# Loading the first sixteen token rows of the input in transfers of 64 partitions instead of 32, with the first four rows asked for in two parts

## The chip, the core and the metric

The kernel runs on one core of a Trainium2 chip. A core has TensorE (PE, matrix products into PSUM), VectorE (DVE), ScalarE (ACT), GpSimd (POOL) and SyncE (SP, which here does nothing but issue transfers). Each engine runs its own instructions strictly in the order in which they stand, and waits on semaphores for the others. Transfers between HBM and SBUF run on 16 DMA engines that SP's and POOL's transfers share. The metric is the device time of one execution in microseconds (us).

## What is computed

The reference is a block of two parts over 2048 tokens of 448 channels, in float32: an S4D state space layer (a long convolution whose kernel K is built from complex exponentials) and an MLP that mixes tokens, each behind an adaptive layer norm:

```python
x = A_u                                            # (1, 2048, 448)
mod = (_silu(c) @ w_mod).reshape(1, 6, 1, -1)      # sa, ca, ga, sb, cb, gb
h = _layernorm(x) * (1 + ca) + sa
# S4D: dt = exp(log_dt), A = -exp(log_A_real) + 1j*A_imag, C = (C_real + 1j*C_imag)*dt
#      K = 2 * real(sum_n C * exp(A * dt * pos)); y = causal convolution of h with K, + h*D_skip
x = x + ga * S4D(h)
h = _layernorm(x) * (1 + cb) + sb
x = x + gb * (W2 gelu(W1 h^T + b1) + b2)^T
```

## The kernel before

The work has three stages. The first, some 300 us, builds the convolution kernel for 28 groups of 16 channels (56 half groups `s`), two halves `s` per group; in windows of eight half groups, beside it, the input is normalised and taken through two stages of a Fourier transform. The second multiplies and transforms back. The third is the MLP, in which PE is busy without a gap.

The parameters of the first 128 channels go through `first_chain` (on DVE, ACT and POOL): it makes exponents and phases, splits each into a rounded float32 part and a rest (`split`: a cast and a subtraction, on POOL or DVE), and SP copies the pieces into the tiles `lex` (exponents, four tiles) and `lph` (phases, three tiles) that PE multiplies with a table `tab`. `direct(ha, lex, r, g)` (L911) is one such copy of 32 KB into rows r to r+32 of tile g. The later parameters go through DRAM: `chain(q)` stores its splits to `pars` (L404) and `load_up` (L616) and `load_lo` (L620) read them back into `lex` and `lph` by group. L620 takes two of the three parameters, so that its source has an outermost extent of two.

In window 0 PE makes the exponents of half groups 0 to 7 (`st_exponents`, L630, into PSUM `xe` and `xg`), ACT takes exp of them (L659). Then, per half group, `st_phase` (PE, L630), sines on ACT (L692 to L698), products with the magnitudes on POOL (`G`, L700 and L701) and DVE (`E`, L702 to L706), and 64 small products of `G` and `E` on PE (`st_kgen`, L727). PE's phases for half group s+2 go into the PSUM tile that DVE has finished reading for s (L706).

The input `A_u` is read once as `xt`: partition p holds 16 consecutive tokens (rows 0 to 15 of the tile), each of 448 floats. `x_load(r0, n)` (L310) brings rows r0 to r0+n: rows 0 to 3 from POOL in `first_chain`, rows 4 to 7 from SP behind the parameters, rows 8 to 11 and 12 to 15 in the half groups 1 and 2, one half of the partitions from SP and one from POOL. DVE takes mean and variance of each row (`u_stats`, L527). In window 8 PE multiplies the rows with a table (L555), DVE writes the results to one of three `yt` tiles (L558, two instructions to a tile) and SP stores each tile to `yu_d` (L560); a `yt` tile can be written again when its store has landed.

SP's queue also carries the modulation weights (`wm_load`, L337, 784 KB each). It is in the written order up to half group 8; behind that a scheduler orders SP's transfers, while the other four engines keep the order of the code throughout. At most eight of SP's transfers are under way: each takes one of eight semaphores in turn, and SP waits until the transfer eight places ahead has landed.

Of the kernel before, what the change touches and what calls it, by code (L numbers as in the profile page):

```python
# [21 lines left out]
L, D, N, F = 2048, 448, 256, 1792  # L22
# [210 lines left out]
def tile_adaln_s4d_mixer(ctx, tc, i, out):  # L233
    nc = tc.nc
    x = i["A_u"][0]
# [17 lines left out]
    with ExitStack() as es:  # L253
        V, S, G, T = nc.vector, nc.scalar, nc.gpsimd, nc.tensor
# [50 lines left out]
        xt = xp.tile([P, 16, D + 2], F32, name="xt")  # L305

        def x_load(r0, n, eng=nc.sync):
            for g in range(4):
                to = xt[32 * g : 32 * g + 32, r0 : r0 + n, 0:D]
                (nc.sync if r0 > 7 and g < 2 else eng).dma_start(to, x.rearrange("(s n h r) d -> h s n r d", s=2, h=2, r=16)[g // 2, g % 2, :, r0 : r0 + n])  # L310


        mg = cg.tile([P, 2, P], BF16, name="mg")
# [9 lines left out]
        lex = [cg.tile([P, N], F32R, name=f"lex{k}") for k in range(4)]  # L323
# [21 lines left out]
        for q in range(4):  # L345
            r = slice(32 * q, 32 * q + 1)
# [542 lines left out]
        def first_chain():  # L889
            cr, ci, a, aim = (raws[0][nm] for nm in ("A_C_real", "A_C_imag", "A_log_A_real", "A_A_imag"))  # L890
            xa, ya, s, t, u, ph, p64 = (
                qp.tile([P, N], F32, tag=nm, name=nm) for nm in ("xa", "ya", "s", "t", "u", "ph", "p64")
            )
# [3 lines left out]
            def split(eng, src):  # L897

                hl = room.pop()
                eng.tensor_copy(hl[:, 0].bitcast(F32R), src)  # L900
                eng.tensor_tensor(hl[:, 1].bitcast(F32R), src, hl[:, 0], ALU.subtract)
                return hl
# [6 lines left out]
            def direct(hl, tile, r, g):  # L909

                nc.sync.dma_start(tile[g][r : r + 32].bitcast(F32), hl[16 * g : 16 * g + 16])  # L911
# [18 lines left out]
            ha = split(G, a)  # L930
            tt(ya, ya, xa, ALU.mult)
            ts(t, s, 2.0**-40, 2.0**80, ALU.is_lt, ALU.mult)
            stt(p64, t, 1.0, s, ALU.max, ALU.mult)
            for g in range(4):
                direct(ha, lex, 0, g)
                if g < 3:
                    direct(ha, lex, 64, g)
            x_load(0, 4, G)
            S.activation(u, ya, AF.Square)
            S.activation(u, u, AF.Ln, bias=1.0)  # L940
            S.activation(p64, p64, AF.Ln)
# [12 lines left out]
            hs = split(V, s)  # L954
            for g in range(4):
                direct(hs, lex, 96, g)
                if g == 2:
                    direct(ha, lex, 64, 3)
            tt(ph, ph, w, ALU.subtract)
            hp = split(G, ph)  # L960
            direct(hp, lph, 0, 0)
# [9 lines left out]
            tt(xa, xa, u, ALU.subtract)  # L971
            hl = split(G, p64)
            direct(hl, lph, 64, 0)
            hc = split(V, xa)
            direct(hc, lph, 96, 0)
            store(ha, (0, 1), (1, 1))
# [3 lines left out]
            store(hc, (2, 0))  # L980

        first_chain()
        par_load(1, par_names[2:4])
        for g in (1, 2):
            load(g, False)
        x_load(4, 2)
        x_load(6, 2)
        wm_load(1, wm_slot(1))
        remainder()
# [254 lines left out]
        n = pieces[0]  # L1244
# [47 lines left out]
        for k in range(NP + 1):  # L1292

            n = NP + k
# [27 lines left out]
            if k in (2, 4):  # L1322
                r = k // 2 - 1
# [13 lines left out]
    with ExitStack() as es:  # L1337
        es.enter_context(tc.manual_schedule(engines={ENG.PE, ENG.Activation, ENG.DVE, ENG.Pool}))
        V, S, G = nc.vector, nc.scalar, nc.gpsimd
# [167 lines left out]
        for t in range(16):  # L1507
            ss = slice(t * P, (t + 1) * P)
            xt = ru.tile([P, D], F32, tag="x2", name="x2")
            nc.sync.dma_start(xt, x2_d[ss])  # L1510
            o = pacc.tile([P, D], F32, tag="acc", name="o")
            for kh in range(2):
                n = 32 + 2 * t + kh
# [38 lines left out]
```

## Time and profile before

| | us |
|---|---|
| median of three runs | 665.27 |
| lowest, highest | 664.42, 666.83 |
| the profiled execution, as timed | 667.08 |
| its span in the profile | 665.3 |
| what lies around the span | 1.78 |
| TensorE's granted clock, mean | 0.991 |

The profile is of one execution. The span counts from its first instruction. Rows of a timeline give start, duration, engine, line, operation, tiles and count, and in brackets the idle time of the engine ahead of it with what ended it; rows of the chain give start, duration and what the end was waiting for there. "SPq" is SP's queue of transfers: the duration is that of issuing, not of the transfer.

### The profile page before, as it was taken

Reading aid. Unit: us, or ns where it says so; the run is one execution under the profiler, and the core shown is the slowest. Engines: PE = TensorE matmul, PEld = TensorE weight load, DVE = VectorE, ACT = ScalarE, POOL = GpSimd, SP = SyncE. Lnnn points to the kernel's source line nnn. Section 1 sums busy time; section 2 is a strip of 40 time slices with the busy share of each in tenths; the row PEclk is TensorE's granted clock in tenths of the full one; section 3 lists DMA queues with packets and bytes.
Section 4 is the critical chain, followed back from the end, with each engine's and each line's share of the span. In section 5 each row is a group of like instructions: output and inputs, shape, how many; then the busy total and the mean of one; then the engine's idle time right before and its main releaser. Section 6 shows DMA issues by size and latency. Waiting matters only on the chain.

```text
span 665.3 us, 19255 instructions
## 1 busy us (share of the span) xinstructions
PE 614.8 (92%) x7686; PEld 445.0 (67%) x7686; DVE 445.5 (67%) x850; ACT 441.1 (66%) x828; POOL 269.8 (41%) x349
## 2 busy tenths in 40 slices
PE   1868999999998999989999899999999999999997
PEld 0534555445455565655655567788999999999997
DVE  8996899889895686859766678787522553333331
ACT  6978598999989999999678588886222532222220
POOL 7884679579499778787564000000000000000000
PEclk9999999999999899999999999999999999999999
DMA  6695647599684467576688999936664265555540
GB/s 160 191 220 146 220 171 243 223 219 285 199 292 152 132 140 207 162 199 202 204 275 273 253 245 248 230 112 203 179 182 142 66 192 163 165 161 163 160 119 29
DMA packets 99602, 125.16 MB, mean 188 GB/s; under 512 B 13780, under 2 KB 81144, under 8 KB 99512
## 3 DMA queue, kind: packets, MB, share of 16 engines
q1 hardware_dynamic: 98568, 121.30, 64.1%
q0 software_dynamic: 944, 2.62, 1.7%
q8 instruction: 61, 1.00, 0.7%
q14 instruction: 29, 0.24, 0.1%
HBM read 88.53 MB, written 34.87 MB: 185 GB/s over the span
## 4 chain that ended last, share of the span: by engine, by line
PE 64%; ACT 11%; DMA 8%; DVE 7%; issue 5%; POOL 4%; SPq 1%; ACTq 0%; POOLq 0%; DVEq 0%
PE o L1518 7%; PE o L1520 7%; PE o L1519 7%; PE xe L630 6%; PE acc L1355 6%; PE acc L1357 6%; PE acc L1356 6%; PE kg L727 5%; PE xg L630 4%; DMA w<-in_B_w_dram 3%; PE vv L858 3%; ACT mag L659 2%; DMA v_d<-vt 2%; PE kx L835 2%; POOL G L700 2%
## 5 line engine op out<-in xcount | busy, mean ns | idle before, releaser
L218 ACT CAST whi<-w 128x896 fp32r<-128x896 f32 x64 | 59.7, 938 | 136.2 <-PE o L1519 82.6
L227 DVE TENSOR_TENSOR wlo<-w,whi 128x896 fp32r<-128x896 f32 x64 | 68.1, 1086 | 40.8 <-ACT whi L218 40.8
L700 POOL TENSOR_TENSOR G<-mag,gs 128x512 f32<-128x512 f32 x56 | 71.9, 1283 | 37.9 <-ACT gs L696 37.9
L1355 PE MATMUL acc<-h3h,whi 128*128 128x448 f32 x224 | 83.0, 371 | 2.3 <-ACT h3h L1428 1.1
L1356 PE MATMUL acc<-h3l,whi 128*128 128x448 f32 x224 | 81.1, 362 | 0.6 <-DVE h3l L1429 0.4
L1518 PE MATMUL o<-uh,whi 128*128 128x448 f32 x224 | 81.3, 363 | 0.0
L1357 PE MATMUL acc<-h3h,wlo 128*128 128x448 f32 x224 | 81.3, 363 | 0.0
L1520 PE MATMUL o<-uh,wlo 128*128 128x448 f32 x224 | 81.2, 362 | 0.0
L1519 PE MATMUL o<-ul,whi 128*128 128x448 f32 x224 | 80.6, 360 | 0.0
L727 PEld LDWEIGHTS kg<-E,G 128*32 128x32 f32 x3584 | 54.7, 111 | 35.7 <-issue 20.6
L727 PE MATMUL kg<-E,G 128*32 128x64 f32 x3584 | 64.8, 222 | 9.0 <-issue 6.4
L701 POOL TENSOR_TENSOR G<-mag,gs 128x512 f32<-128x512 f32 x56 | 71.9, 1284 | 0.0
L630 PE MATMUL xg<-tab,lph 64*128 64x512 f32 x112 | 62.1, 555 | 6.4 <-DVE E L706 4.5
L630 PE MATMUL xe<-tab,lph 64*128 64x512 f32 x112 | 62.3, 557 | 0.6 <-ACT xg L698 0.3
L1523 DVE TENSOR_TENSOR y<-o,x 128x448 f32<-128x448 f32 x16 | 10.0, 624 | 78.9 <-PE o L1520 78.9
L680 POOL TENSOR_TENSOR m<-mag,w 128x512 f32<-128x512 f32 x53 | 55.7, 1051 | 4.2
L1355 PEld LDWEIGHTS acc<-h3h,whi 128*128 128x128 f32 x224 | 42.0, 188 | 15.1 <-ACT h L1427 2.8
L1356 PEld LDWEIGHTS acc<-h3l,whi 128*128 128x128 f32 x224 | 41.9, 187 | 4.2 <-DVE h3l L1429 0.9
L1520 PEld LDWEIGHTS o<-uh,wlo 128*128 128x128 f32 x224 | 42.1, 188 | 3.2
L1357 PEld LDWEIGHTS acc<-h3h,wlo 128*128 128x128 f32 x224 | 42.0, 188 | 3.2
L1519 PEld LDWEIGHTS o<-ul,whi 128*128 128x128 f32 x224 | 41.9, 187 | 2.9
L702 DVE TENSOR_TENSOR E<-m,xe 128x512 f32<-128x512 f32 x53 | 36.1, 682 | 11.3 <-issue 3.3
(249 smaller groups left out, 1405.6 us busy)
## 6 DMA issues: line engine op xcount, KB each, us to landing
w<-in_B_w_dram SPq DMA_DIRECT2D x64, 224.0 KB
w<-in_B_w_dram SPq DMA_DIRECT2D x32, 448.0 KB
yu_d<-yt SPq DMA_DIRECT2D x16, 448.0 KB
yi<-yu_d SPq DMA_DIRECT2D x32, 224.0 KB
us_d<-uo SPq DMA_DIRECT2D x16, 448.0 KB
u<-us_d SPq DMA_DIRECT2D x64, 112.0 KB
v_d<-vt SPq DMA_DIRECT2D x32, 224.0 KB
vt<-v_d SPq DMA_DIRECT2D x14, 448.0 KB
```

The lines of the kernel that those rows point to most:

```text
L218: self.nc.scalar.copy(hi, w)
L227: eng.tensor_tensor(lo, w, hi.bitcast(F32), ALU.subtract)
L630: T.matmul(out[k], lhs[r], rhs[r], start=start, stop=stop)
L700: G.tensor_tensor(Gt[:, 1], mg_, v32(sg), ALU.mult)
L701: G.tensor_tensor(Gt[:, 0], mg_, v32(cg_), ALU.mult)
L727: T.matmul(kg[32 * q : 32 * q + 32, m], Gt[:, c, d], E[:, c, d], start=h == 0 and c == 0 and m == 0, stop=h == 1 and c == 1, skip_group_ch ...
L1355: nc.tensor.matmul(acc[f], hi[:, fs], h3h[:, r], start=r == 0, stop=False)
L1356: nc.tensor.matmul(acc[f], hi[:, fs], h3l[:, r], start=False, stop=False)
L1357: nc.tensor.matmul(acc[f], lo[:, fs], h3h[:, r], start=False, stop=r == 15)
L1518: nc.tensor.matmul(o, hi[:, ks], uh[kh][:, k], start=kh == 0 and k == 0, stop=False)
L1519: nc.tensor.matmul(o, hi[:, ks], ul[kh][:, k], start=False, stop=False)
L1520: nc.tensor.matmul(o, lo[:, ks], uh[kh][:, k], start=False, stop=kh == 1 and k == 6)
```

## The change

`x_load` makes two transfers of 64 partitions instead of four of 32; the tokens that land in each partition are the same. Rows 0 to 3, asked for in one call before, are asked for as rows 0 and 1 at the old place and rows 2 and 3 behind `hl = split(G, p64)`, POOL's last split. The copies of the first split `ha` into `lex` tile 3 (rows 0 and 64) both go out among the copies of `hs` (row 96); one of them stood ahead of these.

```diff
         def x_load(r0, n, eng=nc.sync):
-            for g in range(4):
-                to = xt[32 * g : 32 * g + 32, r0 : r0 + n, 0:D]
-                (nc.sync if r0 > 7 and g < 2 else eng).dma_start(to, x.rearrange("(s n h r) d -> h s n r d", s=2, h=2, r=16)[g // 2, g % 2, :, r0 : r0 + n])
+            for h in range(2):
+                to = xt[64 * h : 64 * h + 64, r0 : r0 + n, 0:D]
+                (nc.sync if r0 > 7 and h == 0 else eng).dma_start(to, x.rearrange("(n h r) d -> h n r d", h=2, r=16)[h, :, r0 : r0 + n])
...
-            for g in range(4):
+            for g in range(3):
                 direct(ha, lex, 0, g)
-                if g < 3:
-                    direct(ha, lex, 64, g)
-            x_load(0, 4, G)
+                direct(ha, lex, 64, g)
+            x_load(0, 2, G)
...
             for g in range(4):
                 direct(hs, lex, 96, g)
-                if g == 2:
-                    direct(ha, lex, 64, 3)
+                if g in (1, 2):
+                    direct(ha, lex, 64 * g - 64, 3)
...
             hl = split(G, p64)
             direct(hl, lph, 64, 0)
+            x_load(2, 2, G)
```

On SP near the start, the copies into `lex` (lex_142 to lex_145 are tiles 0 to 3; the row of two for lex_144 is its copies of `ha`, the single rows of lex_142 and lex_143 are those of `hs`):

```order
 L911 DMA lex_143<-wm_79 32x1x256 x2
 L911 DMA lex_144<-wm_79 32x1x256 x2
-L911 DMA lex_145<-wm_79 32x1x256
 L911 DMA lex_142<-wm_79 32x1x256
 L911 DMA lex_143<-wm_79 32x1x256
+L911 DMA lex_145<-wm_79 32x1x256
 L911 DMA lex_144<-wm_79 32x1x256
```

The copy of `hs` into tile 0 moves up one place, that of `ha` into tile 3 goes back two.

On SP some twenty places on, the input rows 4 to 7 (2x448), the weights (wm_79) and the first halves of rows 8 to 11 and 12 to 15 (4x448), with the phases that are read back for later groups:

```order
-L310 DMA xt<-in_A_u_dram 32x2x448 x8
+L310 DMA xt<-in_A_u_dram 64x2x448 x4
 L337 DMA wm_79<-in_w_mod_dram 112x4x448
-L310 DMA xt<-in_A_u_dram 32x4x448 x2
+L310 DMA xt<-in_A_u_dram 64x4x448
 L616 DMA lph_139<-pars_57 32x256
 L620 DMA lph_139<-pars_57 64x1x256
-L310 DMA xt<-in_A_u_dram 32x4x448 x2
+L310 DMA xt<-in_A_u_dram 64x4x448
```

Twelve transfers become six; what stands between them stays.

On SP in window 8, where the scheduler orders, the stores of the second chain's splits (pars_58 from `hl`), the stores of `yt`, and loads for later:

```order
 L404 DMA pars_58<-hl 128x512 x2
+L291 DMA A_log_A_real<-in_A_log_A_real_dram 64x128 x2
+L616 DMA lex_142<-pars_58 32x256
 L560 DMA yu_d<-yt 128x896
 L404 DMA pars_58<-hl 128x512
-L560 DMA yu_d<-yt 128x896
-L616 DMA lex_142<-pars_58 32x256
+L616 DMA lex_143<-pars_58 32x256
+L560 DMA yu_d<-yt 128x896
+L620 DMA lex_142<-pars_58 64x1x256
```

Two loads from `pars_58`, which need the stores of it that stand just ahead to have landed, now stand ahead of the first and second store of `yt`; loads of raw parameters for the last chain (L291) have come forward from a place some twenty rows on.

## Prediction

> **What bounds the kernel now.** I read the page first, then the chain of waits from 0 to 80 us, then the timelines of DVE, POOL, SP and PE over the same time, and last the DMA engines by stretches. The page's busy times and its chain:
>
> ```profile
> PE 614.8 (92%) x7686; PEld 445.0 (67%) x7686; DVE 445.5 (67%) x850; ACT 441.1 (66%) x828; POOL 269.8 (41%) x349
> PE 64%; ACT 11%; DMA 8%; DVE 7%; issue 5%; POOL 4%; SPq 1%; ACTq 0%; POOLq 0%; DVEq 0%
> ```
>
> PE sets the whole, but the change lies where PE does not: its transfers are issued in the first 40 us. What it is worth is what still stands of a shift when PE, behind that stage, carries it to the end. The chain of the start:
>
> ```profile
> 12.43 0.59 SPq L911
> ...
> 13.07 1.86 DMA lex<-wm
> 14.93 0.78 PE xg L630
> ...
> 15.77 7.44 ACT mag L659 x15
> ...
> 29.83 0.66 DVE E L705
> 30.49 0.61 DVE E L706
> ...
> 44.71 4.38 issue
> ```
>
> The copy of `hs` into tile 0 is issued at 12.43 and lands at 14.93; ACT's exponentials start with it. At 29.83 the chain goes over from ACT to DVE. At 44.71 stands the largest wait of the stage: PE stops for 4.38 us in the middle of 64 equal products and no semaphore shows. DVE's rows of the same stretch, and two further on:
>
> ```profile
> 10.61 0.42 DVE L901 TENSOR_TENSOR wm<-s,wm 128x256 fp32r<-128x256 f32 x1
> ...
> 14.85 1.15 DVE L971 TENSOR_TENSOR xa<-xa,u 128x256 f32<-128x256 f32 x1
> ...
> 27.09 0.67 DVE L702 TENSOR_TENSOR E<-m,xe 128x512 f32<-128x512 f32 x1
> ...
> 33.89 0.69 DVE L702 TENSOR_TENSOR E<-m,xe 128x512 f32<-128x512 f32 x1 [0.41 <-ACT xe L695]
> ...
> 45.80 0.68 DVE L706 TENSOR_TENSOR E<-wm,xg 128x512 f32<-128x512 f32 x1
> ...
> 74.94 1.27 DVE L558 SCALAR_TENSOR_TENSOR yt<-pu,mod 128x448 f32<-128x448 f32 x2
> ...
> 108.40 1.28 DVE L558 SCALAR_TENSOR_TENSOR yt<-pu,mod 128x448 f32<-128x448 f32 x2 [0.79 <-DMA yu_d<-yt]
> ```
>
> No row between 4.24 and 33.89 has a bracket: DVE works without a gap there, so what ACT gains ahead of 29.83 reaches nobody unless DVE gets faster too.
>
> **The start.** `hs` is split at 11.03 (10.61 and 0.42), yet its copy is issued at 12.43: SP is at its older copies.
>
> ```profile
> L911 SPq DMA_DIRECT2D lex<-wm x12: 567/590/725, 7.0 to 14.4; - x12
> DMA  0003897979993989999997212227614999999992
> 20.00:25.00 5.00, 5.00 (x17) 2.72 (x17) 4.86 (x8) 4.97 (x10) 4.69 (x8) 1.00 0.91 320
> ```
>
> The first is the group of these twelve issues, median 0.59 us; one goes back behind `hs`, so its first copy leaves about 0.6 us earlier. The second is the DMA engines' busy share in 40 slices of 0 to 25 us: full up to 13.1 us, at a fifth from 13.75 to 16.9. Half of the first four input rows, 0.46 MB, moves out of the full part into the idle one, and the copy may land sooner than the 1.86 us of the chain. At 320 GB/s, the last row's rate and the best of this stage, these bytes are 1.4 us, of which I take 0.7. So ACT starts 0.6 to 2.0 us earlier; I take 1.3. The copies into tile 3 go later by one or two places, but of ACT's sixteen exponentials, 7.44 us, the last four need it, some 5 us after the first: no cost.
>
> POOL's side:
>
> ```profile
> 6.91 2.27 POOL L310 DMA_DIRECT2D xt<-in_A_u_dram  x4
> ...
> 13.42 0.78 POOL L901 TENSOR_TENSOR wm<-p,wm 128x256 fp32r<-128x256 f32 x1
> 14.17 0.42 POOL L675 TENSOR_TENSOR w<-mag 128x16 f32<-128x16 f32 x1
> 14.66 1.06 POOL L680 TENSOR_TENSOR m<-mag,w 128x512 f32<-128x512 f32 x1
> 16.92 0.24 POOL L675 TENSOR_TENSOR w<-mag 128x16 f32<-128x16 f32 x1 [1.20 <-ACT mag L659]
> ...
> 32.35 1.11 POOL L310 DMA_DIRECT2D xt<-in_A_u_dram  x2
> 72.87 0.40 POOL L398 CAST hl<-ph 128x256 fp32r<-128x256 f32 x1 [0.80 <-DMA pars<-hl]
> ```
>
> Two issues cost 1.11 (half of the first row is 1.14). At the old place they leave a hole, since the cast of `ph` waits for DVE anyway. At the new one they stand ahead of the product at 14.66, which then ends at 16.85, and the 1.20 us of idle time ahead of 16.92 hide that. Without that cover it would be 1.1 us on POOL, and DVE's first E product has its operand from here only at 27.09, so nothing would show. One DVE row profits: L971 took 1.15 beside POOL's product at 14.66 and ends with it, where the same size takes 0.42 at 10.61. With transfers issued there instead, 0.73 us of DVE's unbroken row is saved, if the product, now later, does not hold up another DVE instruction for as long. Bounds 0 and 0.73 each; I take 0.7, because the next DVE instructions are small ones. By 31 us the shift is thus -0.7, not -1.3.
>
> The Trainium skill has a rule that speaks against this edit. SBUF — State Buffer, "SBUF: two separate sides", warns that a transfer issued from GpSimd stalls while VectorE runs two-port operations, since GpSimd then can't write descriptors; its example is 620 ns that become 3100. By that rule the two issues among L971 and its neighbours could hold POOL for some 5 us more, an estimate from that page's figures, and the sum would be up to 4 us higher. No row here shows it: the 1.11 us at 32.35 lie beside DVE's E products and the 2.27 at 6.91 beside its first chain, so I give it no chance of its own.
>
> Rows 2 and 3 are asked for 7 us later. Their use is the first row below, the time of POOL's eight transfers to landing, median 5.1 us, ends the second:
>
> ```profile
> 25.33 0.57 DVE L527 BATCH_NORM_STATS2 st<-xt 128x6 f32<-128x448 f32 x1
> xt<-in_A_u_dram POOLq DMA_DIRECT2D x8, 224.0 KB, 5.1
> ```
>
> Issued by 15.3 they are there at about 20.4, 5 us ahead.
>
> **SP's middle, and PE's stop.** Halving the transfers of rows 4 to 15:
>
> ```profile
> 26.54 6.09 SPq L310 DMA_DIRECT2D xt<-in_A_u_dram  x8
> 32.67 0.43 SPq L337 DMA_DIRECT2D wm<-in_w_mod_dram  x1
> ...
> 42.43 0.31 SPq L337 DMA_DIRECT2D wm<-in_w_mod_dram  x1
> ...
> 67.36 0.93 SPq L404 DMA_DIRECT2D pars<-hl  x2
> 68.66 0.32 SPq L560 DMA_DIRECT2D yu_d<-yt  x1
> ...
> 72.11 0.32 SPq L616 DMA_DIRECT2D lex<-pars  x1
> ...
> 87.26 1.61 SPq L291 DMA_DIRECT2D A_C_real<-in_A_C_real_dram  x2
> ...
> 92.47 1.60 SPq L291 DMA_DIRECT2D A_A_imag<-in_A_A_imag_dram  x2
> ```
>
> Eight issues took 6.09 us, most of it waiting for one of the eight semaphores. Four take about half, so the weights at 32.67 leave at about 29 and, with two fewer transfers in between, those at 42.43 between 36 and 40. Nobody waits for any of these: the bytes are the same, and from 36 to 50 us the DMA engines are the limit, as the first row below shows with its share of 1.07. So nothing is gained by the earlier issue itself. But PE's stop hangs on it:
>
> ```profile
> 39.00:42.00 3.00, 1.82 (x68) 1.33 (x68) 2.93 (x8) 3.00 (x8) 2.24 (x3) 1.00 1.07 210
> 49.09 0.31 PE L727 MATMUL kg<-E,G 128*32 128x64 f32 x6 [4.38 <-issue]
> q8 instruction: 1, 0.02, 4.3%
> ```
>
> The last row is the DMA queue from 46 to 48 us: one packet of instructions, and the answers for each two microseconds from 34 to 46 have no row of that queue. PE ran out of instructions at 44.71 and got them behind the input rows. Without the stop PE would have waited for DVE's L706 up to 46.48 (45.80 and 0.68), so at most 2.6 us are to be had. If the fetch waits behind the bytes that were asked for before it, the time at which PE resumes belongs to the DMA engines and not to PE: then the -0.7 is lost in the stop. I take PE to resume at 49.1 as before, a shift of 0; the ends are -3.3 (no stop and the 0.7 kept) and +3.8 (784 KB of weights at the row's 210 GB/s now ahead of the fetch).
>
> By DMA: Bandwidth & Descriptors, "Queues, rings and completion order", in the Trainium skill, each DMA engine changes between queues packet by packet, so a fetch would wait for single packets, the stop would have another cause and its end would move with PE: the sum would be 0.7 lower. The absence of the queue from 34 to 46 speaks against it.
>
> **SP in window 8.** The scheduler now puts a load of `lex`, which reads what the first store at 67.36 wrote, ahead of the first store of `yt`. Before, that load left at 72.11, as soon as the store had landed (POOL at 72.87 waits for the other of the two), while the `yt` store had left at 68.66. Now the `yt` store leaves at 72.11 + 0.32, 3.8 us later. It is 448 KB: 1.4 us at 320 GB/s and 1.86 us of latency from the chain's row, so it lands at about 75.8 (at the 210 GB/s of the full stretch above 76.5). DVE's fourth pair at 74.94 writes the same buffer. So DVE loses 0.9 us there, between 0 (the first store lands a microsecond earlier) and 1.6. Behind it on SP, the other three stores of splits and of `yt` slip by 1 to 3 us, and POOL's casts that need the buffers; DVE's fifth pair at 78.25 has no need of them before.
>
> What comes back: of the eight small loads from 87.26 to 94.07, four now go earlier, and the `yt` stores behind them with less in front. DVE's row at 108.40 waits 0.79 us for such a store. I take that wait to vanish: -0.8, bounds 0 and -0.8.
>
> **The sum**, against the profiled execution of 667.08 us (span 665.3 and 1.78 around it): -0.7 at the start, +0.7 in PE's stop, +0.9 at 75 us, -0.8 at 108 us: +0.1, so 667.2 there. The median of the three runs is 1.81 lower, at 665.27; I take the difference over: 665.4 us.
>
> **The rivals.**
>
> ```profile
> 30.00:33.00 3.00, 1.81 (x43) 1.29 (x47) 3.00 (x6) 1.61 (x4) 3.00 (x4) 0.93 0.44 109
> ```
>
> *The stream of transfers moves up* (0.18). For it: while SP waits, the DMA engines are at 0.44 between 30 and 33 us, and six transfers fewer close that gap. Then the fetch is early, PE resumes at up to 46.48 - 0.7, the store at 67.36 lands early enough for `yt`, and -2.6 to -3.3 stays: 662.4. Against it: the engines are full from 36 to 50.
>
> *Weights ahead of the instructions* (0.15), the one that ends slower. If the second 784 KB are issued before PE asks for instructions, its stop grows by up to 3.8 us. DVE's wait at 75 is then hidden in it and 0.8 comes back at 108: +3.0 at the far end, +2.2 with four fifths of the weights in front, 667.5. It decides from an issue of those weights ahead of about 40 us.
>
> *SP's new order costs and gives nothing back* (0.15): +0.9 to +1.6, as the lost time returns at no `yt` store: 666.4. *Nothing moves* (0.15): copy and store land when the DMA engines let them, 665.3. My forecast has the remaining 0.37.
>
> **The numbers.** A measurement of this kernel tells about 0.3%, 2.0 us, from no change. Faster by more is the first rival, 0.18; slower by more the second, 0.15; the other three, 0.67, lie within. Both far cases are too likely together to leave out, so the range reaches to the middle of each, from 662.4 to 667.5.
>
> **What would show it.** Right: the first copy of `hs` issued near 11.8 and ACT's exponentials starting 0.6 to 2 us earlier; DVE still without a gap to about 33 and its E products for half group 0 at 26.4, not 27.09; PE's stop in the same 64 products, ending near 49; the first `yt` store behind a `lex` load at about 72 and a bracket on DVE's fourth L558 pair; none on the pair at 108. Wrong: a stop that is gone or twice as long, rows 2 and 3 of the input that DVE waits for near 25 us, or POOL's two issues at 14 us taking several microseconds.

## The result, and the profile after

The changed kernel is slower, where no measurable change was forecast. Medians of runs in turns on one chip:

| | changed | before |
|---|---|---|
| median of six runs, us | 670.60 | 666.05 |
| lowest, highest | 669.14, 672.83 | 664.42, 667.85 |
| profiled execution, its span | 669.14, 667.4 | 667.08, 665.3 |

The ratio is 1.0059, with an interval from 1.0037 to 1.0081: 4.6 us more, against a forecast of 665.4 and a range that ended at 667.5. The two profiled executions lie only 2.1 us apart, so their comparison can show about half of the loss. Ratios with intervals compare executions that ran in turns and leave out the few that were far slower (the traced execution of `best_before`, below, took 1921.88 us), so a ratio need not be that of the two medians.

The busy times of the engines and the shares of the chain that ended last, from the page of the changed kernel:

```profile
PE 620.4 (93%) x7686; PEld 447.2 (67%) x7686; DVE 443.2 (66%) x850; ACT 440.8 (66%) x828; POOL 269.8 (40%) x347
PE 66%; DMA 8%; ACT 7%; POOL 7%; DVE 6%; issue 4%; SPq 1%; POOLq 0%; ACTq 0%; DVEq 0%
```

The chain from 10 to 50 us, in its trace:

```profile
11.94 0.59 SPq L911
...
15.16 0.57 SPq L911
15.78 3.95 DMA A_C_real<-in_A_C_real_dram
...
20.12 1.23 DVE xa L414
...
21.63 1.24 DVE ya L414
...
29.95 0.67 DVE E L702
...
42.62 2.03 issue
```

The first copy of `hs` leaves at 11.94 instead of 12.43, as forecast. But the chain no longer goes from there to ACT. It stays in SP's queue to its end, passes into a load of `A_C_real` that was not in the chain before, and comes to DVE, whose first E product starts at 29.95 instead of 27.09. DVE's timeline of that stretch, in the changed kernel:

```profile
14.96 0.42 DVE L970 TENSOR_TENSOR xa<-xa,u 128x256 f32<-128x256 f32 x1
...
16.09 1.01 DVE L876 TENSOR_SCALAR dt<-dt 128x3 f32<-128x3 f32 x1
...
18.45 0.24 DVE L882 COPY scb<-sc 112x128 f32<-112x128 f32 x1
19.75 0.34 DVE L412 TENSOR_SCALAR xa<-A_C_real 128x256 f32<-128x256 f32 x1 [1.05 <-DMA A_C_real<-in_A_C_real_dram]
20.12 1.23 DVE L414 SCALAR_TENSOR_TENSOR xa<-A_C_real,xa 128x256 f32<-128x256 f32 x1
21.27 0.33 DVE L412 TENSOR_SCALAR ya<-A_C_imag 128x256 f32<-128x256 f32 x1
21.63 1.23 DVE L414 SCALAR_TENSOR_TENSOR ya<-A_C_imag,ya 128x256 f32<-128x256 f32 x1
...
77.07 1.28 DVE L558 SCALAR_TENSOR_TENSOR yt<-pu,mod 128x448 f32<-128x448 f32 x2 [0.40 <-PE pu L555]
...
108.68 1.87 DVE L558 SCALAR_TENSOR_TENSOR yt<-pu,mod 128x448 f32<-128x448 f32 x3
```

And the same place in DVE's timeline of the kernel before:

```profile
16.70 0.16 DVE L876 TENSOR_SCALAR dt<-dt 128x3 f32<-128x3 f32 x1
...
18.34 0.24 DVE L882 COPY scb<-sc 112x128 f32<-112x128 f32 x1
18.51 0.28 DVE L412 TENSOR_SCALAR xa<-A_C_real 128x256 f32<-128x256 f32 x1
18.82 0.43 DVE L414 SCALAR_TENSOR_TENSOR xa<-A_C_real,xa 128x256 f32<-128x256 f32 x1
19.17 0.37 DVE L412 TENSOR_SCALAR ya<-A_C_imag 128x256 f32<-128x256 f32 x1
19.57 0.43 DVE L414 SCALAR_TENSOR_TENSOR ya<-A_C_imag,ya 128x256 f32<-128x256 f32 x1
```

At L882 DVE is where it was (18.45 against 18.34): the 0.73 us that L970 saved are gone again at L876, which takes 1.01 us instead of 0.16 beside the POOL product (L680) that now runs from 15.88 to 17.08. Then it waits 1.05 us for `A_C_real`, and each of the two L414 takes 1.23 us instead of 0.43. POOL's rows of the changed kernel say why:

```profile
14.24 1.19 POOL L310 DMA_DIRECT2D xt<-in_A_u_dram  x2
...
20.02 1.05 POOL L680 TENSOR_TENSOR m<-mag,w 128x512 f32<-128x512 f32 x1
...
21.53 1.05 POOL L680 TENSOR_TENSOR wm<-mag,w 128x512 f32<-128x512 f32 x1
```

Each L414 starts 0.10 us after a product of POOL and ends 0.28 us after it has ended. By the Trainium skill (SBUF — State Buffer, "SBUF: two separate sides") the port that VectorE and GpSimd share is an exclusive lock: whichever starts first holds it for its whole instruction. The rows agree, with 1.23 us beside a 128x512 product of POOL and, in before, 0.43 where none runs (POOL has only its 1x112 copies and a 128x16 product there); the late load moved DVE's instructions onto POOL's products. The warning of the Trainium skill (SBUF — State Buffer, the same section) about transfers issued from GpSimd, weighed in the prediction, did not show: the two issues took 1.19 us.

The load is late because of what stands ahead of it in the engines. Issue and landing (first and last of the sixteen parts), read from the completion events of the two traces, in us:

```
                        before               after
rows 0, 1 (POOL)        6.9 (all four rows)   7.05,  7.67 -> 11.77
rows 2, 3 (POOL)                             14.24, 14.83 -> 18.12, 19.15
A_C_real (SP)           15.73 -> 17.87       15.78 -> 18.81 to 19.73
```

Before, `A_C_real` was there 0.6 us ahead of its use at 18.51. Behind 448 KB of input rows it took 3.95 us instead of 2.14.

Behind 30 us, PE's largest stop of the stage in the changed kernel's PE timeline:

```profile
44.65 1.71 PE L727 MATMUL kg<-E,G 128*32 128x64 f32 x54 [2.03 <-issue]
```

And the stretch from 30 to 33 us in its windows (the columns: length, then busy time and count of PE, PEld, DVE, ACT and POOL, granted clock, DMA share, GB/s):

```profile
30.00:33.00 3.00, 0.76 (x1) 0.28 (x1) 2.97 (x7) 0.19 (x1) 2.34 (x3) 0.53 1.08 232
```

The stop comes in other products than before (behind the tenth of 64 of the third half group, not behind the 58th of the fourth) and is 2.03 us long, not 4.38. So a part of the start's loss is given back: of 2.86 us at the first E product 1.23 are left at 57 us. And the DMA engines, at 0.44 before, are at 1.08 from 30 to 33 us: SP's stream did move up. SP's rows:

```profile
28.68 0.70 SPq L337 DMA_DIRECT2D wm<-in_w_mod_dram  x1
29.43 0.60 SPq L310 DMA_DIRECT2D xt<-in_A_u_dram  x1
...
39.52 0.79 SPq L337 DMA_DIRECT2D wm<-in_w_mod_dram  x1
...
72.21 0.33 SPq L616 DMA_DIRECT2D lex<-pars  x1
72.63 0.38 SPq L560 DMA_DIRECT2D yu_d<-yt  x1
```

Weights leave at 28.68 instead of 32.67 and 39.52 instead of 42.43; the first `yt` store leaves at 72.63 instead of 68.66, behind the `lex` load.

To follow a shift through the kernel, the same DVE instruction is sought in two traces and the difference of its starts taken. This is worked out from DVE's timelines, against the first trace of before, in us:

```
trace                 first E product   at 57 us   at 349 us   at the end
before, second             -0.4           -1.3        0.0         +1.2
before, third              +1.8           +1.1       +1.8         +0.7
after                      +2.9           +1.2       +2.1         +1.7
after, second              +2.3           +1.6       +1.8         +1.9
after, third               +2.8           +1.4       +2.3         +1.0
place                      +1.4           +6.0       +4.6         +3.4
merge                      +0.6           +2.5       +0.9         -0.6
merge, second              +1.1           +2.7       +2.7         +5.1
late                       -0.5           +1.2       +2.1         +0.7
late_hold                  -0.2           +3.5       +4.0         +4.8
late_spread                -0.2           +0.2       +1.2          0.0
after_spread               +2.1           +0.4       +0.9         +1.2
before_spread              +2.5           +2.7       +3.3         +4.1
before_x12                 -0.4           -3.1       +0.7         -0.2
late_spread_x12            +3.2           +2.9       +2.3         +2.7
the same, second           -0.2           -4.4       -1.9         -3.4
ac_first_spread            +0.1           -0.3       -1.0         -1.9
```

The names are those of the experiments below. The traces of before lie up to 2 us apart, so only what all traces of a kernel have in common is read from this table; verdicts come from the ratios. At the first E product the five traces with the `A_C` loads behind rows 2 and 3 (changed, `place`, `after_spread`) are 1.4 to 2.9 us late; the others lie between -0.5 and +1.1, except for three: the third of before, `before_spread` and the first of `late_spread_x12`. The last two wait for an `A_C` load as well, 0.67 and 0.69 us, so a kernel without the new place of rows 2 and 3 can lose its start in a single execution too.

### The profile page after: what moved, and what is told of

The parts are those of the page before. It is cut to its first block, busy times and chain, and to the rows that moved or that the text cites. A ratio compares the mean times of both kernels' runs of the same rounds, so it can differ in the third digit from the quotient of the medians.

```text
span 667.4 us, 19241 instructions
## 1 busy us (share of the span) xinstructions
PE 620.4 (93%) x7686; PEld 447.2 (67%) x7686; DVE 443.2 (66%) x850; ACT 440.8 (66%) x828; POOL 269.8 (40%) x347
## 4 chain that ended last, share of the span: by engine, by line
PE 66%; DMA 8%; ACT 7%; POOL 7%; DVE 6%; issue 4%; SPq 1%; POOLq 0%; ACTq 0%; DVEq 0%
PE o L1518 7%; PE o L1520 7%; PE o L1519 7%; PE xe L630 6%; PE acc L1355 6%; PE acc L1356 6%; PE kg L727 6%; PE acc L1357 6%; PE xg L630 3%; POOL G L700 3%; POOL G L701 2%; PE vv L858 2%; PE kx L835 2%; DMA w<-in_B_w_dram 2%; PE y L765 2%
## 5 line engine op out<-in xcount | busy, mean ns | idle before, releaser
L727 PEld LDWEIGHTS kg<-E,G 128*32 128x32 f32 x3584 | 56.6, 114 | 32.4 <-issue 18.6
L727 PE MATMUL kg<-E,G 128*32 128x64 f32 x3584 | 66.3, 227 | 6.1 <-issue 4.3
L630 PE MATMUL xg<-tab,lph 64*128 64x512 f32 x112 | 63.8, 570 | 5.3 <-DVE E L706 1.6
L630 PE MATMUL xe<-tab,lph 64*128 64x512 f32 x112 | 64.2, 574 | 3.5 <-DVE E L703 3.3
L680 POOL TENSOR_TENSOR m<-mag,w 128x512 f32<-128x512 f32 x53 | 55.9, 1055 | 4.1
L692 ACT ACTIVATE ab<-xe 128x512 f32<-128x512 f32 x56 | 33.8, 603 | 18.5 <-PE xe L630 11.4
```

Of the source, the lines that this page charges most:

```text
L630: T.matmul(out[k], lhs[r], rhs[r], start=start, stop=stop)
L727: T.matmul(kg[32 * q : 32 * q + 32, m], Gt[:, c, d], E[:, c, d], start=h == 0 and c == 0 and m == 0, stop=h == 1 and c == 1, skip_group_ch ...
```

## The experiments

Expectations name theories by letters: A, rows 2 and 3 delay the `A_C` loads at the start; B, SP's new order in window 8; C, the granted clock; D, input row 8 arrives late because of the two engines that carry L620; E, the clock, where the 64-partition transfers alone are slow; F, PE's stop is a fetch of instructions that waits behind bytes.

**Which part of the change costs.** Beside the changed kernel again, `place` has only the new places and orders and keeps transfers of 32 partitions; `merge` has only the transfers of 64; `late` is the changed kernel with rows 2 and 3 asked for two products of POOL later, behind the `A_C` loads.

```diff
# place: on the changed kernel            (merge: the same lines the other way round, on the kernel before)
-            for h in range(2):
-                to = xt[64 * h : 64 * h + 64, r0 : r0 + n, 0:D]
-                (nc.sync if r0 > 7 and h == 0 else eng).dma_start(to, x.rearrange("(n h r) d -> h n r d", h=2, r=16)[h, :, r0 : r0 + n])
+            for g in range(4):
+                to = xt[32 * g : 32 * g + 32, r0 : r0 + n, 0:D]
+                (nc.sync if r0 > 7 and g < 2 else eng).dma_start(to, x.rearrange("(s n h r) d -> h s n r d", s=2, h=2, r=16)[g // 2, g % 2, :, r0 : r0 + n])
# late: on the changed kernel
             direct(hl, lph, 64, 0)
-            x_load(2, 2, G)
...
                 if s == 0 and e == 3:
+                    x_load(2, 2, G)
                     for r in range(4):
```

> The changed kernel unchanged, as the measure for the three kernels beside it on the same chip. Theory A (the start): rows 2 and 3 of the input, asked for at 14.2 us, fill the transfer engines just when DVE's A_C_real load is asked for, DVE starts the second chain 2.9 us late, and what PE's shorter stop does not give back stays. It expects +3.5 to +5 us over the kernel before, and in the profile again a wait of about 1 us of DVE for A_C_real near 19 us with L414 near 1.2 us twice. Theory B (SP's order in window 8): the shift of the start is lost in PE's stop and the first yt store, 4 us later behind a lex load, costs. It expects the same total, with the lag of DVE growing after 68 us. Theory C (the clock): PE's granted clock of 0.66 to 0.69 between 30 and 50 us (0.83 to 0.98 before) is the cost; it expects the same low clock in the same places.

> Only the new places: rows 0 and 1, then rows 2 and 3, and the new order of the copies, with transfers of 32 partitions as before; SP's order in window 8 is then that of the kernel before. Theory A: DVE waits for A_C_real near 18.5 us, E's first product starts 2 to 3 us later than before (27.1), and the time is 2 to 4.5 us above the kernel before. Theory B: DVE may wait there as well, but the time is within 1 us of the kernel before, since PE's stop takes it up. Theory C: the time follows PE's granted clock between 30 and 60 us.

> Only the transfers of 64 partitions: the four rows in one call at the old place, the copies in the old order; SP's order in window 8 is then that of the changed kernel. Theory A: no wait for A_C_real, E's first product at 27.1 or sooner, time within 1.5 us of the kernel before. Theory B: the first yt store near 72 us, a bracket on DVE's L558 pairs near 75, and 3 to 5 us above the kernel before. Theory C: the time follows PE's granted clock between 30 and 60 us.

> The changed kernel with one edit: rows 2 and 3 are asked for by POOL about 4 us later, behind its second magnitude product (L680), so that A_C_real and A_C_imag are ahead of them; SP's order is that of the changed kernel throughout. Theory A: DVE has no gap at 19 us, its first E product comes at 26.4 instead of 29.95, ACT keeps its 1.6 us, and 3 to 5 us of the loss are gone: from 1 us below the kernel before to 1 above. Theory B: as slow as the changed kernel, +3.5 to +5 us. Theory C: as slow as the changed kernel unless PE's granted clock goes up as well.

| | median, us | ratio to before | interval |
|---|---|---|---|
| after_again | 671.13 | 1.0075 | 1.0047 to 1.0103 |
| place | 671.46 | 1.0080 | 1.0050 to 1.0109 |
| merge | 671.08 | 1.0069 | 1.0043 to 1.0095 |
| late | 668.76 | 1.0051 | 1.0026 to 1.0077 |

Each half of the change costs as much as the whole; undoing the start's part alone leaves most of the loss. So there are two costs, and they don't add. `place` has SP's order of before in window 8: theory B is not needed for the loss. At its start DVE waits for the same load (DVE's timeline of `place`), and its first E product is 1.4 us late:

```profile
19.55 0.29 DVE L412 TENSOR_SCALAR xa<-A_C_real 128x256 f32<-128x256 f32 x1 [1.76 <-DMA A_C_real<-in_A_C_real_dram]
```

Behind that its PE stops for longer than before's (PE's timeline of `place`), so that its loss is not the start's alone; why the stop is longer is open:

```profile
53.83 0.43 PE L727 MATMUL kg<-E,G 128*32 128x64 f32 x6 [5.63 <-issue]
```

`merge`, which leaves rows 0 to 3 at the old place, waits at the start too, which theory A had not expected (its DVE timeline):

```profile
19.05 0.29 DVE L412 TENSOR_SCALAR xa<-A_C_real 128x256 f32<-128x256 f32 x1 [1.40 <-DMA A_C_real<-in_A_C_real_dram]
```

Here the load is not slow but is asked for late, at 16.83 instead of 15.73, and lands in 2.20 us. SP's second `lex` copy, issued beside the two transfers of 448 KB for rows 0 to 3, landed at 14.27 instead of 12.51, and SP, which needs its semaphore for the tenth copy, stood until then. Its first E product is 0.6 us late (in its second trace the wait is 1.84 us, and the product 1.1 late).

In `late` there is no loss at the start: no wait ahead of L412, the first E product at 26.64. But DVE waits elsewhere. Its timelines have, in `late`:

```profile
18.35 0.28 DVE L412 TENSOR_SCALAR xa<-A_C_real 128x256 f32<-128x256 f32 x1
...
26.64 0.67 DVE L702 TENSOR_TENSOR E<-m,xe 128x512 f32<-128x512 f32 x1
...
47.69 0.63 DVE L527 BATCH_NORM_STATS2 st<-xt 128x6 f32<-128x448 f32 x1 [5.20 <-DMA xt<-in_A_u_dram]
```

in `merge`:

```profile
49.00 0.63 DVE L527 BATCH_NORM_STATS2 st<-xt 128x6 f32<-128x448 f32 x1 [5.51 <-DMA xt<-in_A_u_dram]
```

and in the kernel before:

```profile
43.74 0.63 DVE L527 BATCH_NORM_STATS2 st<-xt 128x6 f32<-128x448 f32 x1 [0.82 <-DMA xt<-in_A_u_dram]
```

This is row 8, which comes from SP for one half of the partitions. The sixteen parts of that transfer end at (us; of the two transfers of before and `place` the second is shown):

```
             issued   parts 1 to 14 by   last two
before       33.68        42.5           42.7, 43.6
place        32.87        42.2           42.6, 43.1
after        29.43        39.5           43.5, 44.6
merge        30.97        41.3           45.2, 48.9
late         30.47        42.9           46.5, 47.6
late_hold    30.98        43.3           48.0, 48.1
late_spread  31.09        40.6           41.5, 42.8
```

In `merge`, `late` and the changed kernel fourteen parts are there about as early as in before, or up to 3 us earlier, and the last comes 5 to 8 us behind them. The completion of L620, whose source has an outermost extent of two, has two late parts. By the Trainium skill (DMA: Bandwidth & Descriptors, "Why a DMA increments its semaphore by 16 and not by 1") a transfer uses the largest number of engines up to 16 that divides the outer extents, here two. The events agree: two parts of sixteen. So two engines have all bytes of L620 beside their share of everything else.

Which L620 stands in row 8's way can be read from the same events. It is hardly the third: in every kernel of the table in which L620 was not spread it was issued behind row 8's transfer and landed after it (31.49 and 49.7 in the changed kernel). The first two leave two engines behind the others. In the changed kernel their last parts land at 28.6 and 31.4, and in what is issued behind them the last part trails the fourteenth: in the weights by 4.0 us (41.2), in row 8 by 5.2. In before the two land as late (29.1 and 32.3), but there SP needs the second one's semaphore for the last of the eight transfers of rows 4 to 7 and stands from 29.9 to 32.3 us until it is free. The weights and row 8 leave only then, and their last parts trail by 1.6 and 1.1 us. With four transfers fewer SP comes to that semaphore only behind weights and row 8 (31.49, the third L620 itself). In `place`, with eight transfers, the two trail by 1.1 and 0.9. No run has this step by itself.

In the changed kernel itself row 8 lands at 44.6 and its use comes at 45.99, late already by the start: the first cost covers the second.

**Is it L620, and in what way?** `late_hold` keeps L620's place behind the rows (the third group's parameters are read behind rows 12 to 15); `late_spread` makes two transfers of 32 partitions of it, so that all engines carry it. `merge` and before were profiled once more.

```diff
# late_hold: on late
-            if s % 2 == 0 and 0 < s and s // 2 + 2 < NG:
+            if s % 2 == 0 and 2 < s and s // 2 + 2 < NG:
...
             if s in (1, 2):
                 x_load(4 + 4 * s, 4, G)
+            if s == 2:
+                load(3, False)
# late_spread: on late, in load_lo
-            nc.sync.dma_start(t[64:128], src[1:3])
+            if g < 8:
+                for k in (1, 2):
+                    nc.sync.dma_start(t[32 + 32 * k : 64 + 32 * k], src[k])
+            else:
+                nc.sync.dma_start(t[64:128], src[1:3])
```

> The kernel before, for a second trace of it. If the first trace is typical, PE's stop of some 4 us without a releaser stands near 45 us again and DVE waits under 1 us for row 8 of the input (L527 near 43.7). If the stop varies from execution to execution, it is shorter here or in another set of products, and then part of what separates one execution from another lies there.

> The kernel with transfers of 64 partitions alone, for a second trace: its first profiled execution took 666.8 us, the median of its others is 671.1. Theory D (row 8): the wait of DVE for row 8 of the input, 5.5 us in the first trace, is as long or longer here, and an execution at 671 us has 3 to 5 us more in that wait or in PE's stop. Theory E (the clock): the waits are as in the first trace, and PE's granted clock is lower.

> The kernel with rows 2 and 3 behind the second magnitude product, and in addition the third load of lph (L616 and L620 into lph_139) asked for behind rows 12 to 15 instead of ahead of them. Theory D: row 8 is late because that L620, on two of the sixteen transfer engines, is asked for 2 to 3 us earlier than before and shares them with row 8; here row 8 has landed by 44 us instead of 47.6, DVE waits under 2 us for it instead of 5.2, and the time is 1 to 3 us lower than with rows 2 and 3 late alone, unless PE now waits for lph_139 (its load then lands near 50). Rival (the size): a transfer of 64 partitions is late by itself; row 8 lands at 47 to 49 as before and the time stays.

> The kernel with rows 2 and 3 behind the second magnitude product, and in addition the second load of each pair of the first eight groups (L620) as two transfers of 32 partitions, one for each parameter, which go over all sixteen engines instead of two. Theory D: the stragglers are gone, the sixteen parts of each transfer land within 1.5 us of one another, row 8 has landed by 42 us, DVE has no wait over 1 us there, PE's stop is under 2.5 us, and the time is 2 to 5 us below the kernel with rows 2 and 3 late alone, that is at or below the kernel before. Rival (the size): row 8's last part stays 5 us behind its first, and the time is within 1 us of the kernel with rows 2 and 3 late alone. Rival (SP): the added issues of 0.5 us hold SP, and the time is up to 3 us higher.

`late_spread` took 666.23 us, 0.9996 (0.9975 to 1.0017): with both causes away the loss is away, and its interval does not touch that of `late`. DVE's timeline of `late_spread`, at row 8:

```profile
42.93 0.63 DVE L527 BATCH_NORM_STATS2 st<-xt 128x6 f32<-128x448 f32 x1 [0.74 <-DMA xt<-in_A_u_dram]
```

And its PE timeline:

```profile
47.95 0.44 PE L731 MATMUL kg<-E,G 128*32 128x64 f32 x7 [3.88 <-issue]
```

Row 8 waits 0.74 us instead of 5.20, and it still comes in transfers of 64 partitions: their size by itself is not the cause. PE's stop is back to near the 4.38 of before and takes up what the start gained.

`late_hold` took 672.64, 1.0100 (1.0081 to 1.0119): worse. The third L620 left only 1.7 us later (33.98 against 32.29), row 8 still ended at 48.1 (DVE's timeline of `late_hold`), and a new wait came with it (PE's timeline):

```profile
48.22 0.63 DVE L527 BATCH_NORM_STATS2 st<-xt 128x6 f32<-128x448 f32 x1 [4.88 <-DMA xt<-in_A_u_dram]
```

```profile
51.37 0.76 PE L630 MATMUL xe<-tab,lph 64*128 64x512 f32 x1 [1.86 <-DMA lph<-pars]
```

So D in the form that the order of the third L620 decides has failed, in keeping with these events. Spreading the transfers over all engines is what helps.

The profiled executions took 668.32 (before) and 672.58 (`merge`). `merge` has the wait for row 8 in both traces, but their ends lie 5.7 us apart, 4.0 of that behind 349 us, where the change has no instruction. The window from 375 to 400 us of the first trace of `merge`:

```profile
375.00:400.00 25.00, 24.11 (x110) 17.45 (x111) 20.45 (x62) 19.62 (x46) 0.00 (x0) 1.00 1.05 275
```

and of the second:

```profile
375.00:400.00 25.00, 21.13 (x87) 14.58 (x88) 17.38 (x54) 16.84 (x41) 0.00 (x0) 0.93 1.04 248
```

The same kernel had 275 GB/s in one execution and 248 in the other. That is why spans of single executions don't decide here.

**The parts once more, without L620's two engines.** `after_spread` and `before_spread` split L620 as above in the changed kernel and in the one before. `before_x12` asks for rows 12 to 15 two half groups later, to thin out the bytes ahead of PE's fetch; `late_spread_x12` does both.

```diff
# x12
+            if s == 4:
+                x_load(12, 4, G)
             if s in late:
...
-            if s in (1, 2):
-                x_load(4 + 4 * s, 4, G)
+            if s == 1:
+                x_load(8, 4, G)
```

> The changed kernel, with L620 of the first eight groups as two transfers of 32 partitions over all sixteen engines. Theory A and D together: the start stays late (DVE waits for A_C_real near 19 us, E's first product 2 us later than before), only the two stragglers go; DVE is 2 us behind the kernel before at 42 us, and the time is 1 to 3.5 us above the kernel before, some 2 below the changed kernel. Theory D alone (the stragglers are the whole loss): within 1 us of the kernel before.

> The kernel before with the same edit of L620. Theory D: in the kernel before DVE waits only 0.8 us for row 8, so there is little to gain: within 1.5 us of the kernel before, and PE's stop stays at 3 to 4.4 us. If it is 3 us or more faster, the gain with rows 2 and 3 late was the edit's own and says nothing on the change.

> The kernel before with rows 12 to 15 asked for four half groups in instead of two: SP's half behind the load of lph_140, POOL's behind two more products, so that 0.9 MB leave the full stretch of 36 to 46 us. Theory F: PE's stop is a fetch of instructions behind those bytes; its packet then comes by 44 us instead of 46 to 47, the stop shrinks from 4.4 us to under 2, and, since DVE's E products then bound PE at 46.5, the time is 1 to 2.6 us lower. Rival: the stop has another cause, stays at 3 to 4.4 us, and the time is within 1 us.

> The changed kernel with three edits together: rows 2 and 3 behind the second magnitude product, L620 over all engines, rows 12 to 15 four half groups in. Theory F: PE's stop, 3.9 us without the last edit, is under 1.5 us, ACT's and DVE's 0.7 us from the start are no longer lost in it, and the time is 2 to 4 us below the kernel before. Rival: the stop stays, and the time is within 1 us of the kernel before.

| | median, us | ratio to before | interval |
|---|---|---|---|
| after_spread | 670.46 | 1.0063 | 1.0038 to 1.0088 |
| before_spread | 666.41 | 0.9995 | 0.9968 to 1.0022 |
| before_x12 | 670.43 | 1.0053 | 1.0023 to 1.0083 |
| late_spread_x12 | 664.26 | 0.9982 | 0.9956 to 1.0007 |

`after_spread` and `late_spread` differ in one line, the place where rows 2 and 3 are asked for, and by 4.2 us (670.46 and 666.23, from two comparisons) with intervals that don't meet. That is the cost of this place by itself, and `after_spread` is not below the changed kernel, where some 2 us had been expected. In the trace of `after_spread` DVE waits as in the changed kernel, if for less:

```profile
19.27 0.29 DVE L412 TENSOR_SCALAR xa<-A_C_real 128x256 f32<-128x256 f32 x1 [0.51 <-DMA A_C_real<-in_A_C_real_dram]
...
20.30 1.22 DVE L414 SCALAR_TENSOR_TENSOR ya<-A_C_imag,ya 128x256 f32<-128x256 f32 x1
```

The trace holds less than the median: of its +2.1 us at the first E product 0.4 are left at 57 us and 1.2 stand at the end. Where the rest of the 4.2 us falls was not seen.

Before gains nothing from the split of L620, as its row 8 was not late. `before_x12` did what F says at PE: the packet of instructions comes at 40 to 42 us instead of 46 to 48, the stop is gone, and DVE is 3.1 us ahead at 57 us. The other traces bear F out as well: the stop comes in the same one or two places each time, and all 27 such stops of over 0.25 us (nineteen traces, without `best_before`) end 1.3 to 1.7 us after the end of a packet of instructions of 16 KB. PE waits for weights instead (its timeline):

```profile
53.15 0.96 PE L516 MATMUL pm<-wm,scb 112*32 112x448 f32 x8 [2.56 <-DMA wm<-in_w_mod_dram]
```

But the gain is gone by 349 us in its trace, and the median is 3.2 us above before's. Where that goes is open.

**The start from its other side.** `ac_first_spread` leaves rows 2 and 3 where the change puts them and takes the other party out of the way: the `A_C` loads are asked for behind the split of `hs`, ahead of its copies.

```diff
# on after_spread
             hs = split(V, s)
+            par_load(1, par_names[0:2])
...
-            par_load(1, par_names[0:2])
```

> The changed kernel with L620 over all engines, and with the loads of A_C_real and A_C_imag asked for ahead of the four copies of hs instead of behind them; rows 2 and 3 stay where the change has them. Theory A: it is the wait for these two loads that costs; DVE has no gap at 19 us although rows 2 and 3 are in the same place, ACT starts some 1 us later than in the changed kernel, and the time is within 1.5 us of the kernel before, 2 to 4 us under the changed kernel with L620 spread (670.5). Rival (POOL's issues, or the other copies behind rows 2 and 3): the time stays at 2 to 4 us above the kernel before.

> The changed kernel, for a third trace. Theory A: E's first product again at 29 to 30 us, DVE 2 us or more behind the first trace of the kernel before at 57 and at 349 us; an execution at 671 us has 3 to 4 us there. If instead it is 2 us or less behind at 349 us and loses the rest after it, the remainder lies in the weight loads of the last stage and not in the start.

> The kernel before, for a third trace. Theory A: within 1.3 us of its first two traces at 57 and 349 us; an execution at 665 us has gained its 2 us against the first trace behind 349 us or in a shorter stop of PE.

> The kernel with rows 2 and 3 late, L620 spread and rows 12 to 15 later, for a second trace: its median is 664.3 us, its first traced execution 669.9 with a wait for A_C_imag and a stop of 3.25 us. Expected in an execution near 664: no wait for the A_C loads, E's first product at 26.4 to 27, PE's stop under 2 us.

`ac_first_spread` took 667.05, 1.0020 (1.0001 to 1.0039), 3.4 us under `after_spread` across two comparisons; the intervals just touch. Its loads were issued at 11.21 and landed at 13.38, and DVE's wait and the longer L414 are gone (its DVE timeline):

```profile
18.60 0.28 DVE L412 TENSOR_SCALAR xa<-A_C_real 128x256 f32<-128x256 f32 x1
18.91 0.43 DVE L414 SCALAR_TENSOR_TENSOR xa<-A_C_real,xa 128x256 f32<-128x256 f32 x1
...
19.66 0.43 DVE L414 SCALAR_TENSOR_TENSOR ya<-A_C_imag,ya 128x256 f32<-128x256 f32 x1
```

So most of the start's cost is the delay of these two loads, not something else that rows 2 and 3 meet. The 0.2% that stay are hardly more than nothing.

Three more profiled executions took 668.47 (changed), 667.74 (before) and 663.9 (`late_spread_x12`). The third trace of before has one of its L414 beside POOL too, without a wait for the load: DVE itself is 0.6 us later there, and that is enough.

```profile
20.13 1.22 DVE L414 SCALAR_TENSOR_TENSOR ya<-A_C_imag,ya 128x256 f32<-128x256 f32 x1
```

**The best version.** `best_changed` is `late_spread_x12` once more, beside `best_before`, the kernel before with the same two additions and without the change.

> Rows 2 and 3 behind the second product, transfers of 64 partitions, L620 spread, rows 12 to 15 four half groups in; measured a second time beside the next kernel. Theory A, D and F: 1 to 3 us below the kernel before, and 0.5 to 1.5 us below the next one, which is what the change's earlier start is worth when no stop of PE takes it.

> The kernel before with L620 spread and rows 12 to 15 four half groups in. Theory A, D and F: 0 to 2 us below the kernel before. Rival (these two edits lose on the kernel before, as rows 12 to 15 later alone did by 0.5%): 2 to 4 us above it.

They took 664.49, 0.9996 (0.9972 to 1.0021), and 664.52, 0.9976 (0.9953 to 0.9999). So the change without its two costs has no measurable worth; what is gained is from the two additions, and is barely told from nothing.

## Why the prediction was wrong

The step that failed first is the start's term, "-0.7". Part of what it counted came: the `hs` copy at 11.94 (forecast 11.8), ACT's first exponential at 14.17 instead of 15.76, the subtraction L971 of before, which is L970 now, at 0.42 instead of 1.15, POOL's two issues at 1.19 without harm, and no wait for rows 2 and 3. But the 0.73 us were counted almost in full "because the next DVE instructions are small ones", and the small L876 lost them to the moved product: DVE had nothing left at 18.4 us. Then came what the working had not asked. It asked when the moved bytes are needed ("5 us ahead") and not what lands behind them. "Moves out of the full part into the idle one" was true of the 40 slices and hid that the idle part was where `A_C_real` came in, with 0.6 us to spare. "DVE still without a gap to about 33" was the mark by which it would show, and it failed at 19 us: +2.9 instead of -0.7.

In `late` and `late_spread`, without that wait, DVE is 0.95 and 0.69 us ahead at the E product of 33.89, near the size of the forecast, but by luck: their subtraction takes 1.15 us as in before, and the lead comes above all from L418, which misses POOL's products there (0.42 us instead of 1.15).

The second is "Nobody waits for any of these". In before DVE already waits 0.82 us for row 8; the working had the stream of transfers moving up and took it as harmless because the bytes are the same. They are not the same on each engine: two of the sixteen carry L620. Nor were the 6.09 us of the eight issues "most of it waiting": 2.4 us of them were, in one place, for the second L620 to land. By the events this wait let the two engines catch up before weights and row 8 were asked for, and the change moved it behind them: row 8's last part came 5.2 us behind the fourteenth instead of 1.1. In the changed kernel the start covers this, and in `late` it is the whole loss (1.0051, against 0.9996 with L620 spread).

The other terms: PE's stop was taken as pinned at 49.1. It moved to other products and shrank to 2.03 us; of the start's +2.9, 1.2 to 1.6 us are left at 57 us in the three traces. The loss at 75 us, +0.9, did not come although SP's order changed just as said: the first store left at 72.63 (forecast 72.4) and landed at 75.17, and DVE, late itself, had no wait there. The wait of 0.79 us at 108 us is gone, as forecast, and the lag fell from 1.74 to 0.86 us over it.

Of the rivals, the stream that moves up did so and gave no time, and weights ahead of the fetch did not lengthen the stop in the changed kernel. None of them named either cause.

What stays open. The three traces of the changed kernel are 1.8 to 2.3 us behind at 349 us; the medians differ by 4.6. All three traced executions of it (669.14, 669.31, 668.47) lie below its medians and all three of before (667.08, 668.32, 667.74) above theirs, so an untraced part of the loss may be more of the same, but that was not seen. `after_spread` has the same gap between trace and median. How much of the loss of `merge` is row 8 and how much its start was not taken apart. The granted clock (0.980 against 0.991 on the mean of the first pair) was not varied. Its mean over the seven stretches of 3 us from 30 to 51 us is 0.89 in before, 0.67 in the changed kernel, and 0.84 in both `merge` (1.0069) and `late_spread` (0.9996), so there it does not tell a slow kernel from a quick one; what the 0.67 costs the changed kernel is open.

## What to carry to other kernels

When bytes are moved to a later place, list what lands behind them there and its slack, not only who needs the moved bytes; an idle stretch of the DMA engines may be the room of a load that is just in time. Fewer, larger transfers let an issuer that waits for a free semaphore run ahead, and then a transfer that runs on few engines decides when everything behind it is complete. Where undoing a part of a change helps little, undo two: of two costs that cover each other, each alone looks innocent, and here only the pair `late` and `late_spread`, and its mirror `after_spread`, showed both.

## What the runs showed of the hardware

A transfer's completion is that of its slowest part: with L620 on two engines, row 8's other fourteen parts were there 5 to 8 us before the last. PE's stop on instructions fell at one or both of the same two places of the code in every trace that has it, behind the tenth product of the third half group and behind the 58th of the fourth (one product earlier where L620 is spread). Its length, 0 to 5.63 us, went with the packet of instructions: PE resumed 1.3 to 1.7 us after the packet's end each time. And a delay of one microsecond in a load cost DVE 2.9 in the changed kernel's first trace, since behind it two instructions of 0.43 us each met one of POOL's and took 1.23.
